# Attention q products in two 64-row halves, and k, v sums placed by one copy, in a one-core attention and expert-routing kernel

## The chip, the core and the metric

One core of one Trainium2 chip runs the whole program. Its engines have a queue each: TensorE (PE in the rows, PEld for its weight loads), VectorE (DVE), ScalarE (ACT), GpSimd (POOL) and SyncE (SP). They wait for one another by semaphores. The metric is the device time of one execution in microseconds, as the median of several.

## What is computed

Eight batches of 576 tokens with eight heads of 64 columns go through a linear attention without softmax; each head's output row is divided by its root mean square and scaled by `g_norm`. The 4608 rows of 512 columns then go to one of eight experts each (the largest gate logit), in the order of the tokens and up to a capacity of 1152 for an expert; an expert is two products with a ReLU between. Rows beyond the capacity stay zero.

```python
kv = np.einsum('bhsd,bhse->bhde', k, v)               # 8, 8, 64, 64
out = np.einsum('bhsd,bhde->bhse', q, kv)             # 8, 8, 576, 64
rms = np.sqrt(np.mean(out * out, axis=-1, keepdims=True) + 1e-06)
x = (out / rms * g_norm)                              # laid out as 4608 x 512
logits = x @ w_gate                                   # 4608 x 8
expert_idx = np.argmax(logits, axis=1)
gate_w = softmax(logits)[np.arange(N), expert_idx]
...                                                   # dispatch in order of tokens, up to capacity
h = np.maximum(np.einsum('ecd,edf->ecf', disp, w1), 0.0)     # F = 1024
y = np.einsum('ecf,efd->ecd', h, w2)
out[i] = gate_w[i] * y[expert_idx[i], pos[i]]         # for each token that was kept
```

## The kernel before, in words

**Stages.** The first part, to about 100 us, is the attention over the eight batches with the routing of each batch behind it; the first expert's weights are loaded and split in the same stretch. The second part, to the end, is the experts: tiles of tokens are gathered (`xg`, `xm`), turned and cast (`xs`), multiplied by w1 (L566), passed through ReLU into a high and a low f16 part (`hh`, `hl`), multiplied by w2 (L613), and scattered into the output (L643). Each expert product is three terms, high by high, high by low and low by high, for which the weights are split into `w1h`, `w1l`, `w2h` and `w2l` (L411 makes the low parts on DVE).

**Attention, by batch.** `load` (S, the queue of loads) brings k and v in two parts each and q in one. `kv_products` (L752 to 805) sums kᵀv of each head over five chunks of tokens: 40 matmuls (L761) for each half of the heads. They leave head 2i in partitions 0 to 63 and head 2i + 1 in partitions 64 to 127 of one PSUM bank `a`. `apart` copies the bank to `kvs`; `turn` (L785) transposes that, `keep` copies it to `kvt`, and `gates` (L794) multiplies it by the gate weights, so that each head gets eight more columns for the routing. The right operand of the q products is `kv_bd` (L300): four pairs of heads, each a block-diagonal 128x144 matrix (72 columns = 64 of kv and 8 of gates for each head), with zeros off the diagonal that GpSimd writes once, at the start (L700). The diagonal blocks are filled by two `spread` copies (64x4x64 each, one for each half of the partitions) and two small copies of the gate columns (64x4x8).

**Units.** A `unit` (L811 to 830) is one chunk of 128 tokens of one batch, five to a batch, 40 in all. It has two halves of four heads: two matmuls of 128 rows by 144 columns into one bank `op` (L822; in f32 each matmul is two passes), and a copy of the 128x288 result to `o_sb` (L826, recorded at the line of the copy itself, L719 for ACT or L721 for DVE). There are four `op` banks, so two units fit. `squares` (L833 to 850) squares the result on ACT (L843) and sums it on DVE into `ss` (L848). When all five chunks of a batch are summed, `route` makes the root mean square (`vh`, `yi`, `nrt`), the logits, the chosen expert (`ohe`) and the running number of each token in its expert: `place` on PE (L965, `misc<-ohe`), and `enter` into the table of slots (`tab`). After the last batch, `count` (L1042, one product on `misc`) gives the tokens of each expert; the order of the experts and the registers of the later gathers come from it.

**What sets the order.** All this is not issued in the order of the code. `Plan.op` takes, for each operation, the engines that may do it with a length on each ("A", 0.29 and "V", 0.34 for a copy of `kvs`; "T", 0.49 for half a unit), its dependencies, a key, and the rotating buffers (`Ring`) that it takes and uses. `Plan.place` is a list scheduler: it repeatedly takes, over all engines, the operation that can start first by these lengths, ties by key, and so decides both engine and order; `emit` issues the instructions in that order. Where the plan leaves PE idle before an operation, `emit` puts in dummy products (`beside`, L694, one for each 0.31 us of idle time in the plan). A length in the plan therefore changes what is issued where, for all engines. The tiles of the first expert come into the same plan; a second plan orders the rest of the experts.

Of the kernel before, what the change touches and what calls it, by code (L numbers as in the profile page):

```python
# [66 lines left out]
LOAD = 1.41  # L67
QLOAD = 2.75
# [106 lines left out]
def attention_moe_kernel(  # L175
# [124 lines left out]
    for i in range(2):  # L300
        kv_bds.append(cst.tile([P, HH, 2, XW], F32, name=f"kv_bd{i}"))
# [397 lines left out]
    for t in kv_bds:  # L699
        nc.gpsimd.memset(t, 0.0)  # L700
# [44 lines left out]
    def kv_products(b, ts):  # L745
# [30 lines left out]
        def spread(g):  # L776

            return op([("A", 0.29), ("V", 0.34)],
                      lambda e: copy(e, kv2[rows[g], :, g, 0:D], ks.t[rows[g]].rearrange("p (i x) -> p i x", i=HH)), done[0:1],
                      key + 1.5, (kv,), (ks,))  # L780
# [19 lines left out]
        done = [spread(g) for g in range(2)]  # L800
        for g in range(2):
            done.append(op([("A", 0.19), ("V", 0.13)],
                           lambda e, g=g: copy(e, kv2[rows[g], :, g, D:XW],
                                               a3.t[rows[g], 0:H * E].rearrange("p (i g x) -> p i g x", g=2, x=E)[:, :, g]),
                           [o] + done[0:2], key + 2, (kv,), (a3,)))
# [5 lines left out]
    def unit(b, n, ts, kv, ready, oh):  # L811
        c, key = CHUNKS[n], b * C + n
        o_sb, done = oh.t, []
        for half in range(2):
            qh, qd = ts["q", 0]
            ph = new("op")

            def product(e, half=half, qh=qh, ph=ph):
                ph.t = bank("op")
                for i in range(2):  # L820
                    q0 = half * CD + (i * MD * 2 + c * P if c else i)
                    nc.tensor.matmul(ph.t[:, i * 2 * XW:(i + 1) * 2 * XW], lhsT=qh.t[:, q0:q0 + P],  # L822
                                     rhs=kv.t[:, 2 * half + i].rearrange("p g x -> p (g x)"), start=True, stop=True)

            def out_(e, half=half, ph=ph):
                copy(e, o_sb[:, c, half * HH:(half + 1) * HH].rearrange("p h x -> p (h x)"), ph.t[:, 0:4 * XW])  # L826

            o = op(("T", 0.49), product, [qd] + ready, key + half * 0.1, (ph,), (qh, kv))
            done.append(op([("A", 0.29), ("V", 0.37)], out_, [o], key + half * 0.1, (oh,), (ph,)))
        return done  # L830
# [883 lines left out]
```

## Time and profile before

| | us |
|---|---|
| median of 3 runs | 535.31 |
| the three runs | 534.57, 535.31, 536.51 |
| profiled execution, its own time | 536.39 |
| span of its instructions | 534.6 |
| PE busy | 514.1 (96%) |
| DVE busy | 372.1 (70%) |
| ACT busy | 243.8 (46%) |
| POOL busy | 167.6 (31%) |
| mean granted TensorE clock | 0.994 |

All rows come from one profiled execution, whose time lies 1.08 us above the median and 1.8 us above its span. Times in the rows are counted from the start of the span. A matmul of the f32 kind stands as two instructions, so a unit of four matmuls is eight. The dummies are counted as busy PE. Weight loads (PEld) overlap products. A copy of a helper that all stages call has the helper's line, so it is told by the names of its tiles. The idle time before a row is printed with what ended it; `issue` there means that the engine waited for nothing that the trace shows, and `remote` that the releaser isn't known.

### The profile page before, as it was taken

Reading aid. Unit: us, or ns where it says so; the run is one execution under the profiler, and the core shown is the slowest. Engines: PE = TensorE matmul, PEld = TensorE weight load, DVE = VectorE, ACT = ScalarE, POOL = GpSimd, SP = SyncE. Lnnn points to the kernel's source line nnn. Section 1 sums busy time; section 2 is a strip of 40 time slices with the busy share of each in tenths; the row PEclk is TensorE's granted clock in tenths of the full one; section 3 lists DMA queues with packets and bytes.
Section 4 is the critical chain, followed back from the end, with each engine's and each line's share of the span. In section 5 each row is a group of like instructions: output and inputs, shape, how many; then the busy total and the mean of one; then the engine's idle time right before and its main releaser. Section 6 shows DMA issues by size and latency. Waiting matters only on the chain.

```text
span 534.6 us, 11557 instructions
## 1 busy us (share of the span) xinstructions
PE 514.1 (96%) x4456; PEld 356.4 (67%) x4456; DVE 372.1 (70%) x999; ACT 243.8 (46%) x482; POOL 167.6 (31%) x173
## 2 busy tenths in 40 slices
PE   8999898999898999999999999999999999999995
PEld 7998887966464665477546755775587478558743
DVE  4488787998598899999998993768297335104800
ACT  1665587993236526547256252625263353112111
POOL 2001002001524652563265406430743353120012
PEclk8999999999999999999999999999999999999999
DMA  8999999722697893974849645555546132010010
GB/s 309 419 420 421 422 419 417 285 101 99 226 303 144 235 274 65 364 190 138 281 138 276 148 132 184 151 151 163 167 144 140 55 93 44 20 45 23 1 40 33
DMA packets 61806, 102.69 MB, mean 192 GB/s; under 512 B 38508, under 2 KB 38508, under 8 KB 59698
## 3 DMA queue, kind: packets, MB, share of 16 engines
q1 hardware_dynamic: 54144, 70.50, 42.4%
q0 software_dynamic: 7584, 31.38, 16.5%
q8 instruction: 37, 0.61, 0.5%
q14 instruction: 23, 0.19, 0.1%
q10 hardware_dynamic: 18, 0.02, 0.0%
HBM read 73.20 MB, written 20.68 MB: 176 GB/s over the span
## 4 chain that ended last, share of the span: by engine, by line
issue 32%; PE 31%; POOL 13%; DVE 11%; DMA 8%; ACT 4%; POOLq 1%; another core or an unknown queue 1%; DVEq 0%; SPq 0%; ACTq 0%
PE yp L613 10%; PE hp L566 9%; DMA v_sb<-in_v_dram 6%; POOL out_dram L643 4%; POOL pair L499 3%; POOL xm L470 3%; PE op L566 3%; PE op L822 2%; POOL xg L462 2%; DMA xg<-x_dram,gi 2%; PE a L761 2%; DVE am L376 2%; PE misc L694 1%; PE yp L622 1%; ACT sq L843 1%
## 5 line engine op out<-in xcount | busy, mean ns | idle before, releaser
L566 PE MATMUL hp<-xs,w1h 128*128 128x320 f16 (+6 forms) x960 | 134.0, 292 | 3.1 <-DVE hl L574 1.5
L566 PEld LDWEIGHTS <-w1h 128*128 128x128 f16 x1024 | 99.5, 98 | 36.9 <-issue 4.9
L643 POOL DMA_INDIRECT out_dram<-ysb,si x42 | 46.7, 1112 | 162.9 <-ACT ysb L638 157.3
L613 PEld LDWEIGHTS <-hh 128*128 128x128 f16 x560 | 54.4, 98 | 62.8
L571 ACT ACTIVATE hh<-hp 128x320 f16<-128x320 f32 (+7 forms) x64 | 41.0, 640 | 105.4 <-PE hp L566 97.0
L376 DVE TENSOR_REDUCE am<-raw 128x1 f32<-128x512 f32 x112 | 70.5, 674 | 4.9 <-DMA raw<-in_moe_w_dram 4.8
L566 PE MATMUL hp<-xs,w1l 128*128 128x320 f16 (+6 forms) x480 | 71.9, 292 | 0.0
L638 ACT ACTIVATE ysb<-yp,ysc 128x512 f32<-128x512 f32 (+5 forms) x41 | 28.1, 684 | 92.3 <-PE yp L613 88.5
L574 DVE SCALAR_TENSOR_TENSOR hl<-hp,hh 128x320 f16<-128x320 f32 (+7 forms) x64 | 47.5, 742 | 29.2 <-ACT hh L571 26.3
L613 PE MATMUL yp<-w2l,hh 128*128 128x512 f16 x272 | 64.6, 379 | 0.0
L613 PE MATMUL yp<-w2h,hh 128*128 128x512 f16 x272 | 64.4, 379 | 0.0
L613 PE MATMUL yp<-w2h,hl 128*128 128x512 f16 x272 | 64.4, 379 | 0.0
L566 PEld LDWEIGHTS <-w1l 128*128 128x128 f16 x512 | 50.0, 98 | 16.6
L462 POOL DMA_INDIRECT xg<-x_dram,gi x42 | 42.4, 1010 | 49.5 <-DVE gt L475 14.3
L411 DVE SCALAR_TENSOR_TENSOR w2l<-raw,sw,w2h 128x512 f16<-128x512 f32 x64 | 54.1, 886 | 1.0 <-ACT w2h L405 1.0
L628 DVE COPY yt<-yp 128x256 f32<-128x256 f32 (+4 forms) x7 | 2.9, 413 | 72.9 <-PE yp L622 63.6
L411 DVE SCALAR_TENSOR_TENSOR w1l<-raw,sg,w1h 128x512 f16<-128x512 f32 x64 | 52.0, 858 | 0.0
L613 PEld LDWEIGHTS <-hl 128*128 128x128 f16 x280 | 27.2, 98 | 34.1 <-issue 1.8
L499 POOL TENSOR_TENSOR pair<-xm,pair 128x512 f16<-128x512 f32 (+5 forms) x27 | 32.2, 1192 | 42.7 <-ACT pair L495 42.4
L405 ACT ACTIVATE w2h<-raw,sw 128x512 f16<-128x512 f32 x64 | 41.3, 711 | 8.7 <-PE yp L622 7.7
L822 PE MATMUL op<-kv_bd,q_sb 128*128 128x144 f32 x320 | 44.0, 290 | 0.2 <-issue 0.2
L405 ACT ACTIVATE w1h<-raw,sg 128x512 f16<-128x512 f32 x64 | 41.3, 712 | 2.3 <-DVE sg L400 2.3
(230 smaller groups left out, 618.7 us busy)
## 6 DMA issues: line engine op xcount, KB each, us to landing
raw<-in_moe_w_dram SPq DMA_DIRECT2D x64, 512.0 KB
in_sb<-in_k_dram SPq DMA_DIRECT2D x16, 576.0 KB
v_sb<-in_v_dram SPq DMA_DIRECT2D x32, 288.0 KB
q_sb<-in_q_dram SPq DMA_DIRECT2D x8, 1152.0 KB
x_dram<-o_sb POOLq DMA_DIRECT2D x8, 720.0 KB
x_dram<-o_sb POOLq DMA_DIRECT2D x8, 576.0 KB
xg<-x_dram,gi POOLq DMA_INDIRECT x42
out_dram<-ysb,si POOLq DMA_INDIRECT x42
```

Of the source, the lines that this page charges most:

```text
L376: nc.vector.tensor_reduce(out=am()[:, p:p + 1], in_=raw[:, sl(p)], axis=AX.X, op=ALU.max, apply_absolute_value=True)
L405: nc.scalar.activation(wh[:, sl(p)], raw[:, sl(p)], AF.Copy, scale=z["s"])
L411: nc.vector.scalar_tensor_tensor(out=wl[:, sl(p)], in0=raw[:, sl(p)], scalar=z["s"], in1=wh[:, sl(p)], op0=ALU.mult, op1=ALU.subtract)
L462: nc.gpsimd.indirect_dma_start(out=self.xg[i][0:n], out_offset=None, in_=x_dram[0:self.rows, :], in_offset=bass.IndirectOffsetOnAxis(ap=se ...
L499: eng.tensor_tensor(out=pair[0:n, 1], in0=self.xm[i][0:n], in1=pair[0:n, 0], op=ALU.subtract)
L566: nc.tensor.matmul(self.view(hp)[:, v], lhsT=w[:, c, f * P:(f + 1) * P], rhs=x[:, c, u * hw:(u + 1) * hw], start=(t == 0 and c == 0), stop ...
L571: nc.scalar.activation(self.out(self.hh, j), self.view(hp), AF.Relu)
L574: nc.vector.scalar_tensor_tensor(out=self.out(self.hl, j), in0=self.view(hp), scalar=0.0, in1=self.out(self.hh, j), op0=ALU.max, op1=ALU.s ...
L613: nc.tensor.matmul(yp[0:n, 0:DM], lhsT=h[:, j, o:o + n], rhs=w[:, j, :], start=(m == 0), stop=(m == len(self.terms) - 1))
L638: nc.scalar.activation(self.ysb[0:n], yp[0:n, 0:DM], AF.Copy, scale=self.ysc[0:n, i:i + 1])
L643: nc.gpsimd.indirect_dma_start(out=(disjoint.pop() if disjoint else out)[:, :], out_offset=bass.IndirectOffsetOnAxis(ap=self.sidx[0:n, col ...
L822: nc.tensor.matmul(ph.t[:, i * 2 * XW:(i + 1) * 2 * XW], lhsT=qh.t[:, q0:q0 + P], rhs=kv.t[:, 2 * half + i].rearrange("p g x -> p (g x)"), ...
```

## The change

- `kv_bd` is now 128x4x72 without the off-diagonal blocks: head 2i of pair i is in partitions 0 to 63, head 2i + 1 in 64 to 127, as `kvs` has them. GpSimd's memsets of it go.
- The two `spread` copies become one, `whole` (128x4x64). The gate columns are still copied by two.
- A unit is one operation on PE instead of two, planned with 0.87 in place of twice 0.49. It has eight matmuls of 64 rows by 72 columns (16 passes), one of the lower and one of the upper half of the partitions in turn; the lower ones go to one bank, the upper ones to another. Each of the two copies out takes one bank, which now holds every second head, so that its destination in `o_sb` is four pieces of 72 columns.

```diff
+UNIT = 0.87
...
-        kv_bds.append(cst.tile([P, HH, 2, XW], F32, name=f"kv_bd{i}"))
+        kv_bds.append(cst.tile([P, HH, XW], F32, name=f"kv_bd{i}"))
...
-    for t in kv_bds:
-        nc.gpsimd.memset(t, 0.0)
...
-        def spread(g):
-
-            return op([("A", 0.29), ("V", 0.34)],
-                      lambda e: copy(e, kv2[rows[g], :, g, 0:D], ks.t[rows[g]].rearrange("p (i x) -> p i x", i=HH)), done[0:1],
-                      key + 1.5, (kv,), (ks,))
+        def whole(e):
+            copy(e, kv2[:, :, 0:D], ks.t.rearrange("p (i x) -> p i x", i=HH))
...
-        done = [spread(g) for g in range(2)]
+        done = [op([("A", 0.29), ("V", 0.34)], whole, done, key + 1.5, (kv,), (ks,))]
         for g in range(2):
             done.append(op([("A", 0.19), ("V", 0.13)],
-                           lambda e, g=g: copy(e, kv2[rows[g], :, g, D:XW],
+                           lambda e, g=g: copy(e, kv2[rows[g], :, D:XW],
                                                a3.t[rows[g], 0:H * E].rearrange("p (i g x) -> p i g x", g=2, x=E)[:, :, g]),
-                           [o] + done[0:2], key + 2, (kv,), (a3,)))
+                           [o] + done[0:1], key + 2, (kv,), (a3,)))
...
-        o_sb, done = oh.t, []
-        for half in range(2):
-            qh, qd = ts["q", 0]
-            ph = new("op")
-
-            def product(e, half=half, qh=qh, ph=ph):
-                ph.t = bank("op")
-                for i in range(2):
-                    q0 = half * CD + (i * MD * 2 + c * P if c else i)
-                    nc.tensor.matmul(ph.t[:, i * 2 * XW:(i + 1) * 2 * XW], lhsT=qh.t[:, q0:q0 + P],
-                                     rhs=kv.t[:, 2 * half + i].rearrange("p g x -> p (g x)"), start=True, stop=True)
-
-            def out_(e, half=half, ph=ph):
-                copy(e, o_sb[:, c, half * HH:(half + 1) * HH].rearrange("p h x -> p (h x)"), ph.t[:, 0:4 * XW])
-
-            o = op(("T", 0.49), product, [qd] + ready, key + half * 0.1, (ph,), (qh, kv))
-            done.append(op([("A", 0.29), ("V", 0.37)], out_, [o], key + half * 0.1, (oh,), (ph,)))
-        return done
+        o_sb, (qh, qd), phs = oh.t, ts["q", 0], (new("op"), new("op"))
+
+        def product(e):
+            for g in range(2):
+                phs[g].t = bank("op")
+            for i in range(HH):
+                q0 = i // 2 * CD + (i % 2 * MD * 2 + c * P if c else i % 2)
+                for g in range(2):
+                    r = slice(g * D, (g + 1) * D)
+                    nc.tensor.matmul(phs[g].t[:, i * XW:(i + 1) * XW], lhsT=qh.t[r, q0:q0 + P], rhs=kv.t[r, i], start=True,
+                                     stop=True)
+
+        def out_(e, g):
+            copy(e, o_sb[:, c, g::2], phs[g].t[:, 0:HH * XW].rearrange("p (i x) -> p i x", i=HH))
+
+        o = op(("T", UNIT), product, [qd] + ready, key, phs, (qh, kv))
+        return [op([("A", 0.29), ("V", 0.37)], lambda e, g=g: out_(e, g), [o], key + g * 0.1, (oh,), (phs[g],)) for g in range(2)]
```

The new lengths and dependencies give the plan another order in the attention stage; behind it the experts' order is the same row for row, as are the loads' on SP throughout. Three places follow, each kernel's instructions in the order in which the engine gets them.

**Order piece 1**, PE, around the last k, v products of batch 7 (`a<-v_sb_82`) and the units of batch 6 (`kv_bd_160`) and 7 (`kv_bd_161`), before:

```order
L761 MATMUL a<-v_sb_82,in_sb_76 64x64 x20
L694 MATMUL misc<-iota_94 128x128 x3
L785 MATMUL a<-ident,kvs 128x128 x2
L694 MATMUL misc<-iota_94 128x128 x2
L794 MATMUL a<-wgs,kvt 128x32 x2
L694 MATMUL misc<-iota_94 128x128 x2
L822 MATMUL op<-kv_bd_160,q_sb_77 128x144 x20
L822 MATMUL op<-kv_bd_161,q_sb_78 128x144 x10
```

and after:

```order
L760 MATMUL a<-v_sb_82,in_sb_76 64x64 x20
L695 MATMUL misc<-iota_94 128x128 x4
L781 MATMUL a<-ident,kvs 128x128 x2
L695 MATMUL misc<-iota_94 128x128 x2
L818 MATMUL op<-kv_bd_160,q_sb_77 128x72 x16
L790 MATMUL a<-wgs,kvt 128x32 x2
L818 MATMUL op<-kv_bd_160,q_sb_77 128x72 x24
L695 MATMUL misc<-iota_94 128x128 x2
L818 MATMUL op<-kv_bd_161,q_sb_78 128x72 x16
L482 MATMUL x<-ident,xm 128x128 x4
```

Two units of batch 6 moved ahead of batch 7's gate products, and other work of PE now lies between the units of batch 6 and 7.

**Order piece 2**, DVE, around the copies of batch 7's k, v sums (`kvs`, `kv_bd_161`) and batch 6's `vh`, before:

```order
L721 COPY o_sb_231<-op 128x288
L848 TENSOR_REDUCE ss_232<-sq 128x8
L411 SCALAR_TENSOR_TENSOR w1l_175<-raw_173,sg,w1h_174 128x512
L848 TENSOR_REDUCE ss_232<-sq 128x8
L411 SCALAR_TENSOR_TENSOR w1l_175<-raw_173,sg,w1h_174 128x512
L872 TENSOR_SCALAR vh<-ss_232 128x40
L721 COPY kv_bd_161<-kvs 64x4x64
L411 SCALAR_TENSOR_TENSOR w1l_175<-raw_173,sg,w1h_174 128x512 x2
L886 TENSOR_TENSOR nrt<-yi,vh 128x40
L721 COPY kv_bd_161<-a 64x4x8
```

and after:

```order
L843 TENSOR_REDUCE ss_230<-sq 128x8
L720 COPY o_sb_229<-op 128x4x72
L843 TENSOR_REDUCE ss_230<-sq 128x8
L720 COPY o_sb_229<-op 128x4x72
L412 SCALAR_TENSOR_TENSOR w1l_175<-raw_173,sg,w1h_174 128x512
L843 TENSOR_REDUCE ss_230<-sq 128x8
L720 COPY kvs<-a 128x256
L843 TENSOR_REDUCE ss_230<-sq 128x8
L412 SCALAR_TENSOR_TENSOR w1l_175<-raw_173,sg,w1h_174 128x512
L867 TENSOR_SCALAR vh<-ss_230 128x40
```

The copy `kvs` moved from ACT to DVE, ahead of `vh`; DVE's copy into `kv_bd_161` is gone, and more `o_sb` copies lie on DVE there.

**Order piece 3**, PE, around batch 7's `place` (`misc<-ohe` with `upto`) and the count (`misc<-ohe` with `ones`), before:

```order
L965 MATMUL misc<-ohe,upto_123 128x8
L1042 LDWEIGHTS ones_117
L1042 MATMUL misc<-ohe,ones_117 128x8
L613 LDWEIGHTS hl
L613 MATMUL op<-w2h_176,hl 128x512
```

and after:

```order
L960 MATMUL misc<-ohe,upto_123 128x8
L695 MATMUL misc<-iota_94 128x128
L1037 LDWEIGHTS ones_117
L1037 MATMUL misc<-ohe,ones_117 128x8
L695 MATMUL misc<-iota_94 128x128 x2
L614 LDWEIGHTS hh
L614 MATMUL op<-w2l_177,hh 128x512
```

The count, which stood behind four products of hh by w2l, now stands ahead of them and of two dummies.

## Rows read from the trace of the kernel before

**Rows 1.** The page, sections 1 and 2: busy times, and DMA by slice.

```profile
PE 514.1 (96%) x4456; PEld 356.4 (67%) x4456; DVE 372.1 (70%) x999; ACT 243.8 (46%) x482; POOL 167.6 (31%) x173
...
DMA  8999999722697893974849645555546132010010
```

**Rows 2.** Windows of 5 us, its header giving the columns, from 90 us.

```profile
core 0: us, PE busy (x) PEld busy (x) DVE busy (x) ACT busy (x) POOL busy (x), PEclk, DMA share, GB/s
...
90.00:95.00 5.00, 3.17 (x26) 2.79 (x25) 2.79 (x9) 3.23 (x9) 1.54 (x2) 1.00 0.88 352
95.00:100.00 5.00, 5.00 (x42) 4.96 (x41) 4.97 (x15) 5.00 (x16) 0.00 (x0) 1.00 0.87 292
```

**Rows 3.** Timeline, PE: start, length, engine, line, tiles, count, [idle before <-releaser].

```profile
82.05 4.16 PE L822 MATMUL op<-kv_bd,q_sb 128*128 128x144 f32 x32
86.14 1.39 PE L761 MATMUL a<-v_sb,in_sb 128*64 128x64 f32 x40
...
88.20 1.39 PE L761 MATMUL a<-v_sb,in_sb 128*64 128x64 f32 x40 [0.68 <-DMA v_sb<-in_v_dram]
...
92.16 0.44 PE L785 MATMUL a<-ident,kvs 128*128 128x128 f32 x2 [1.71 <-ACT kvs L719]
...
93.17 0.63 PE L794 MATMUL a<-wgs,kvt 128*128 128x32 f32 x4
...
94.17 7.78 PE L822 MATMUL op<-kv_bd,q_sb 128*128 128x144 f32 x60
```

**Rows 4.** Groups by form, 0 to 130 us: count, busy us, mean ns, idle before.

```profile
L822 PE MATMUL op<-kv_bd,q_sb 128*128 128x144 f32 x320 | 44.0, 290 | 0.2 <-issue 0.2
L848 DVE TENSOR_REDUCE ss<-sq 128x8 f32<-128x512 f32 x40 | 26.9, 680 | 1.7 <-ACT sq L843 1.2
L761 PE MATMUL a<-v_sb,in_sb 128*64 128x64 f32 x640 | 23.0, 228 | 2.3 <-DMA v_sb<-in_v_dram 2.2
L719 ACT COPY o_sb<-op 128x288 f32<-128x288 f32 x62 | 23.0, 405 | 9.1 <-PE op L822 8.4
L721 DVE COPY o_sb<-op 128x288 f32<-128x288 f32 x18 | 8.1, 453 | 4.6 <-PE op L822 4.4
...
L411 DVE SCALAR_TENSOR_TENSOR w2l<-raw,sw,w2h 128x512 f16<-128x512 f32 x8 | 6.0, 744 | 0.0
```

**Rows 5.** Timeline, DVE, ACT and PE, 84 to 109 us.

```profile
84.04 0.17 DVE L678 COPY gi<-gidx_tab 128x6 int32 x1 [0.35 <-issue]
...
89.56 0.18 DVE L872 TENSOR_SCALAR vh<-ss 128x40 f32<-128x40 f32 x1
...
91.74 0.37 ACT L719 COPY kvs<-a 128x256 f32<-128x256 f32 x1 [2.40 <-remote]
...
92.14 0.28 DVE L721 COPY kv_bd<-kvs 64x256 f32<-64x256 f32 x1 [2.40 <-ACT kvs L719]
...
93.28 0.40 ACT L719 COPY kv_bd<-kvs 64x256 f32<-64x256 f32 x1
...
106.24 0.69 DVE L489 TENSOR_TENSOR xs<-x,xs 128x512 f16<-128x512 f32 x1
...
108.72 0.81 PE L566 MATMUL op<-xs,w1h 128*128 128x384 f16 x4 [0.18 <-ACT xs L719]
```

**Rows 6.** Timeline, DVE and PE, at batch 7's numbering and count.

```profile
128.83 1.03 PE L613 MATMUL op<-w2l,hh 128*128 128x512 f16 x4
128.86 0.24 DVE L946 TENSOR_REDUCE ohe<-ohe 128x8 f16<-128x48 f16 x1
129.95 0.17 PE L1042 MATMUL misc<-ohe,ones 128*128 128x8 f16 x1
130.16 0.20 DVE L971 TENSOR_TENSOR inc<-misc,ohe 128x40 f32<-128x40 f32 x1 [1.06 <-PE misc L1042]
...
131.70 0.83 PE L694 MATMUL misc<-iota 128*128 128x128 f32 x6
...
146.46 1.90 PE L566 MATMUL hp<-xs,w1h 128*128 128x320 f16 x12 [0.46 <-ACT ysb L638]
```

## What is predicted for the changed kernel

> **What bounds the kernel now.** I read the page's busy times and slices first [rows 1]. TensorE (PE) is busy 514.1 of 534.6 us, but in the attention stage, which the change touches, that is no sign of a bound: dummy products fill its gaps there. The DMA slices stand at 8 and 9 for the first six or seven slices of 13.4 us each, so up to about 90 us loading sets the pace, and work that an engine saves there is hidden by the loads as long as their order stays.
>
> Second, the windows after that [rows 2]. From 95 to 100 us VectorE (DVE) is busy 4.97 and ScalarE (ACT) 5.00 of 5.00 us, PE 5.00 as well, while DMA falls to 0.87. What counts is therefore the end of attention: the last two batches, 6 and 7, whose products are copied out of PSUM, squared, summed and routed by ACT and DVE. After that PE works through the experts with few gaps, so a microsecond there is a microsecond at the end, if the routing of batch 7, which the later gathers wait for, moves along.
>
> Third, the timelines of that end. PE finishes the last k, v products at about 89.6 (88.20 plus 1.39) [rows 3], but ACT's copy `kvs` starts at 91.74, after 2.40 us of waiting whose releaser the trace doesn't know; DVE's `kv_bd` waits 2.40 behind it, and PE's transposes 1.71 [rows 3, 5]. From 94.17 PE runs 60 passes of the q products without a gap [rows 3]. The first expert product starts at 108.72, released by ACT's last `xs` [rows 5]. Batch 7's numbering (`ohe` on DVE) ends at 129.10 (128.86 plus 0.24); DVE then waits 1.06 us for PE, which counts at 129.95 only after four w2l products [rows 6].
>
> **The change part by part.** *The q products.* Before, a unit (128 tokens of a batch) is four matmuls of 144 columns, in f32 two passes each, so eight passes: (7.78 - 0.29) / 59 = 0.127 us from start to start, 1.02 us a unit [rows 3, 4]. After, it is eight matmuls of 72 columns, sixteen passes, each on half of the partitions. No row of before shows such halves, so bounds. The pace of one pass with 128 weight columns doesn't fall with its columns: the 32-column gate products run at (0.63 - 0.28) / 3 = 0.117 us [rows 3]. If the halves don't overlap, a unit takes 16 x 0.117 = 1.87 us. If they overlap fully, 8 x 0.117 = 0.94. The nearest row is the k, v product, which runs on two halves of the columns: (1.39 - 0.22) / 39 = 0.030 us a pass, 0.060 for a pair with 64 weight columns [rows 3, 4]; twice that for 128 columns is 0.12 a pair, 0.96 a unit. I take 0.94, because pairs on halves are shown to overlap there; the plan's new constant, 0.87, is near it. Over 40 units that saves PE 40 x 0.08 = 3.2 us, 30 of them under the loads; at the end the ten units of batches 6 and 7 save 0.8 us, on an engine that waits for ACT and DVE there.
>
> Changing between halves and the whole array costs something too: the k, v products start 0.09 us later than the q products' pace would have it (82.05 + 31 x 0.125 + 0.125 = 86.05, and the row says 86.14) [rows 3]. In the new order the last ten units stand in six groups, twelve changes, about 1.1 us, which takes back the 0.8. The Trainium skill, TensorEngine Tiling (Array Packing), Key Properties, says that changing the tiling mode drains TensorE; that 0.09 us agrees with it, and for the new mode no row shows it.
>
> *The copies out.* They stay 80, of 288 elements each: 0.405 us on ACT, 0.453 on DVE [rows 4]. Their destination falls into four pieces; ACT's `kv_bd` copy, also in four pieces, took 0.40 for 256 elements where `kvs`, in one, took 0.37 [rows 5]. So up to 0.03 each, 20 x 0.03 = 0.6 on two engines at the end, 0.3 us at most, and nothing where the other engine is the later one; I take 0.1. Both copies of a unit now wait for the whole unit, but the last copy of one is no later. Here TensorEngine Tiling (Array Packing), PSUM Bottleneck, in the Trainium skill speaks against the change: tiling makes TensorE faster and leaves the evacuation of PSUM as it is. The windows agree, with ACT and DVE full at 95 to 100 us; by that rule alone the saving would be nought, which is nearly what my sum has.
>
> *k and v placed by one copy.* One copy of each batch goes: 0.28 us on DVE or 0.40 on ACT [rows 5]. Seven lie under the loads. The last is in the count below. The memsets on GpSimd that go stand at the start, beside the first loads: nothing. The order on the queue of loads is the same row for row, so nothing is held up there but by the q load of the last batch, which waits for batch 5's units; they are now mixed with k, v products of about 1.4 us, while transfers are still queued ahead of it. I cost that at nothing; without that cover it would be about 1 us.
>
> *The moved work, at the end.* PE now takes batch 6's first units before batch 7's gate products, and `kvs` of batch 7 is now on DVE (order pieces 1, 2). When does DVE reach it? Before, from its `gi` copy at 84.04 to `vh` at 89.56 it does three w1l, four sums and one `o_sb` copy. After, ahead of `kvs` stand two w1l, four sums and five `o_sb` copies: 4 x 0.45 more, 0.75 less [rows 4, 5], so `kvs` at about 89.56 + 1.05 = 90.6, if the unexplained wait doesn't recur, and at 91.74 if it does.
>
> From there to the end of batch 7's `ohe` DVE has 121 instructions before and 121 after. Leaving: the `kv_bd` copy (0.28), two gate copies (an estimate of 0.2 each, small beside the rest), an `o_sb` copy (0.45), one w2l (0.75): 1.9. Coming: `kvs` (0.37), one sum (0.67), an `xs` cast (as the `xs` row, 0.69), two small ones (0.2 each): 2.1 [rows 4, 5]. So the stretch is 129.10 - 92.14 = 36.96 before [rows 5, 6] and 37.2 after, but begins with `kvs` itself, 0.40 earlier than `kv_bd` did. It ends at 90.6 + 37.2 = 127.8, or at 91.74 + 37.2 = 128.9: 1.3 or 0.2 us earlier.
>
> What is late next? PE's count. Before, it stands behind four w2l products (about 0.86 us) and follows `ohe` by 0.85; after, those four and two dummies are behind it, and the three dummies after the hl products (0.66) are gone [rows 6] (order piece 3). So the count follows `ohe` closely, and what was saved ahead of it is paid behind it: 0.86 + 0.44 - 0.66 = 0.64 more up to batch 7's table, against 0.65 less. PE and routing both shift by about 1.3 or 0.2 us. The first expert product has room: up to the count PE has 129.95 - 108.72 = 21.2 us of work, 1.3 less after, so it may start as late as 108 to 109; from `kvs` to it took 17.0 before, with no more on DVE's queue now, so 107.6 or 108.7.
>
> **The sum.** Profiled execution 536.39 us, span 534.6 and 1.8 around it; it lies 1.1 above the median 535.31. 536.39 - 1.3 + 0.1 = 535.2 or 536.39 - 0.2 + 0.1 = 536.3. The wait of 2.1 us at `kvs` has no cause in the trace, and the three runs differ by 1.9, so it may come and go in either kernel; I take the middle, **535.7 us**, no change: within 0.3% of the median, 533.7 to 536.9, which is about what a measurement of this kernel can tell.
>
> **Rivals.**
> *Faster, 533.5.* The wait is a matter of the old order and goes for good, and batch 6's units, no longer behind batch 7's gates, fill ACT and DVE from 90 on: `kvs` at 89.6, a stretch from there to 126.8, 2.3 earlier, and DVE's wait of 1.06 for the count shrinks to the 0.75 of the w2l moved into it, 0.3, with 0.3 of PE's wait before the rest's products (0.46) [rows 6]: 2.9 in all. For it: both engines idle 2.40 us in before. Against: DVE then has as much work as before.
>
> *Slower by the halves, 541.* The halves don't overlap, so the change doesn't do what it says. PE gets to the end of the ten units at about 96.0 + 10u (91.6 after the transposes, and 4.4 of gates, dummies, transposes and changes of mode), and needs 1.1 more to the first expert product. It decides from u = 1.08, where this passes 107.9; at u = 1.87 the product starts at 115.8, the count at 135.7 after 19.9 us of work, 5.7 late at most, some of it given back in later waits: 541. Against it: the k, v pairs overlap.
>
> *Slower by the order, 537.7.* The wait recurs and PE's path is 1 to 1.5 us longer: more changes of mode than I priced, or the two copies of a unit, released together, hold the four banks longer. DVE and ACT then wait in a stretch where nothing has slack. The point is PE's end of the ten units passing DVE's second `xs` sum, 105 to 107, at a unit of about 1.0.
>
> **Chances.** Forecast 0.45; faster 0.33; slower by the order 0.12, by the halves 0.10. So faster 0.33, same 0.45, slower 0.22. The range takes in the faster rival and the milder slower one, with 0.7 and 0.8 around them for the wait that comes and goes: 532.8 to 538.5; the halves stay out. The forecast's own range is 534.8 to 536.9.
>
> **What would show it.** After's rows should have sixteen q passes a unit within 0.87 to 1.0 us, in pairs; more than 1.08 is the halves. `kvs` on DVE at 90.6 (or 91.7), the first expert product at 107 to 109, the count at 127.9 to 129.3, ACT and DVE still full at 95 to 100, and the DMA slices as before. The prediction is wrong if batch 7's numbering moves more than 2 us, or if the loads end later.

## The result, and the profile after

The changed kernel takes 539.19 us (median of 15 runs, 537.12 to 550.76), the kernel before 535.93 us beside it (15 runs). The ratio of the two is 1.0057, with a 95% interval of 1.0033 to 1.0081: slower by 0.6%, some 3 us. A ratio leaves out runs more than 1.5% above the fastest of their kernel (here two of the 15). Forecast were 535.7 us, no change, and 538.5 as the upper end. The profiled execution took 539.08 us, its span is 537.3, its mean granted clock 1.000.

The page of after, busy times and DMA by slice, against [rows 1]: PE is 5.0 us busier, DVE and ACT are as they were.

```profile
PE 519.1 (97%) x4798; PEld 359.1 (67%) x4798; DVE 373.1 (69%) x996; ACT 243.4 (45%) x477; POOL 167.0 (31%) x171
...
DMA  8999998823588793994839647555645132010010
```

Windows of after, same columns and stretch as [rows 2]. DMA falls earlier, 0.77 in the first of them against 0.88. PE is full from 95 us on as before, DVE and ACT, with 4.47 and 4.28, not quite.

```profile
core 0: us, PE busy (x) PEld busy (x) DVE busy (x) ACT busy (x) POOL busy (x), PEclk, DMA share, GB/s
90.00:95.00 5.00, 3.89 (x56) 3.33 (x54) 3.20 (x6) 2.77 (x7) 2.35 (x3) 1.00 0.77 233
95.00:100.00 5.00, 5.00 (x81) 4.76 (x80) 4.47 (x12) 4.28 (x13) 0.00 (x0) 1.00 0.89 314
```

Timeline of after, PE and one row of DVE (start, length, engine, line, tiles, count, idle before), for [rows 3, 5, 6]. L818 are the q products, L760 the k, v products, L695 dummies.

```profile
11.29 2.08 PE L695 MATMUL misc<-iota 128*128 128x128 f32 x8
...
17.76 0.47 PE L818 MATMUL op<-kv_bd,q_sb 64*128 64x72 f32 x4
...
83.08 2.01 PE L818 MATMUL op<-kv_bd,q_sb 64*128 64x72 f32 x32
...
90.03 1.34 PE L760 MATMUL a<-v_sb,in_sb 128*64 128x64 f32 x31
91.70 0.35 PE L760 MATMUL a<-v_sb,in_sb 128*64 128x64 f32 x4 [0.33 <-issue]
...
93.19 0.29 PE L760 MATMUL a<-v_sb,in_sb 128*64 128x64 f32 x2 [0.39 <-issue]
...
95.16 2.01 PE L818 MATMUL op<-kv_bd,q_sb 64*128 64x72 f32 x32
97.10 0.63 PE L790 MATMUL a<-wgs,kvt 128*128 128x32 f32 x4
97.66 2.90 PE L818 MATMUL op<-kv_bd,q_sb 64*128 64x72 f32 x48
100.49 0.71 PE L695 MATMUL misc<-iota 128*128 128x128 f32 x4
101.13 2.13 PE L818 MATMUL op<-kv_bd,q_sb 64*128 64x72 f32 x32
...
110.55 0.66 PE L567 MATMUL op<-xs,w1h 128*128 128x384 f16 x3
...
148.48 1.76 PE L567 MATMUL hp<-xs,w1h 128*128 128x320 f16 x11 [0.46 <-ACT xs L718]
```

```profile
93.52 0.42 DVE L720 COPY kvs<-a 128x256 f32<-128x256 f32 x1 [0.78 <-PE a L760]
```

The halves do overlap: 48 passes in 2.90 us are (2.90 - 0.28) / 47 = 0.056 a pass, 0.89 for a unit. Yet `kvs` of batch 7 starts at 93.52, released by PE, where 90.6 or 91.7 was forecast; batch 6's first unit starts 1.0 us later than in [rows 3], the first expert product 1.8 later and the rest's first product (`hp`) 2.0 later than in [rows 5, 6].

The 2.7 us between the two spans have three places. 1.4 are there already at the first unit, 17.76 against 16.38 in before (below); one program starts as differently from one execution to the next, as the experiments show. 0.6 come between it and `hp` (130.72 us against 130.08). The last 0.7 come behind `hp`, at one gather of the experts. There DVE waits for `xg` and PE for DVE, 3.27 us against 2.32 at DVE. In e10 and e17 below, which have the new products too, that wait is 2.50 and 2.45, so its longer form doesn't come with them each time. PE's and DVE's rows of before for these places, and then of after:

```profile
9.86 2.08 PE L694 MATMUL misc<-iota 128*128 128x128 f32 x8 [0.19 <-DVE wgs L315]
...
16.38 0.85 PE L822 MATMUL op<-kv_bd,q_sb 128*128 128x144 f32 x5
...
80.34 0.66 PE L822 MATMUL op<-kv_bd,q_sb 128*128 128x144 f32 x4
...
167.41 0.15 DVE L475 TENSOR_SCALAR gt<-xg 128x1 f32<-128x1 f32 x1 [2.32 <-DMA xg<-x_dram,gi]
...
170.39 0.22 PE L391 MATMUL pt_max<-diag,ones_b 128*128 128x128 bf16 x1 [1.55 <-DVE diag L388]
```

```profile
170.31 0.15 DVE L476 TENSOR_SCALAR gt<-xg 128x1 f32<-128x1 f32 x1 [3.27 <-DMA xg<-x_dram,gi]
...
173.29 0.22 PE L392 MATMUL pt_max<-diag,ones_b 128*128 128x128 bf16 x1 [2.49 <-DVE diag L389]
```

### The profile page after: what moved, and what is told of

The parts are those of the page before. It is cut to its first block, busy times and chain, and to the rows that moved or that the text cites. A ratio compares the mean times of both kernels' runs of the same rounds, so it can differ in the third digit from the quotient of the medians.

```text
span 537.3 us, 12232 instructions
## 1 busy us (share of the span) xinstructions
PE 519.1 (97%) x4798; PEld 359.1 (67%) x4798; DVE 373.1 (69%) x996; ACT 243.4 (45%) x477; POOL 167.0 (31%) x171
## 4 chain that ended last, share of the span: by engine, by line
PE 38%; issue 31%; POOL 13%; DVE 10%; ACT 5%; DMA 3%; POOLq 1%; ACTq 0%; SPq 0%
PE yp L614 12%; PE hp L567 9%; PE op L818 5%; POOL out_dram L644 4%; PE a L760 4%; POOL xm L471 3%; POOL pair L500 3%; PE op L567 3%; POOL xg L463 2%; PE misc L695 2%; DVE am L377 2%; DVE w2l L412 2%; DMA xg<-x_dram,gi 1%; DVE hl L575 1%; ACT sq L838 1%
## 5 line engine op out<-in xcount | busy, mean ns | idle before, releaser
L639 ACT ACTIVATE ysb<-yp,ysc 128x512 f32<-128x512 f32 (+5 forms) x41 | 28.1, 684 | 91.7 <-PE yp L614 82.6
L818 PE MATMUL op<-kv_bd,q_sb 64*128 64x72 f32 x640 | 41.5, 276 | 0.0
```

The lines of the kernel that those rows point to most:

```text
L639: nc.scalar.activation(self.ysb[0:n], yp[0:n, 0:DM], AF.Copy, scale=self.ysc[0:n, i:i + 1])
L818: nc.tensor.matmul(phs[g].t[:, i * XW:(i + 1) * XW], lhsT=qh.t[r, q0:q0 + P], rhs=kv.t[r, i], start=True, stop=True)
```

## The experiments

The first question was which part of the change costs the time: the order or the products. The kernels that bear on it, with the dummies in the whole trace (before has 79) and the range of the runs' mean granted clocks (half clock for 10.7 of 537 us makes a mean of 0.99):

| kernel | products | dummies | runs | clock | median us | ratio to before |
|---|---|---|---|---|---|---|
| after | halves | 90 | 15 | 0.972 to 1.000 | 539.19 | 1.0057 [1.0033, 1.0081] |
| e5, after again | halves | 90 | 6 | 0.984 to 0.993 | 541.49 | 1.0094 [1.0076, 1.0111] |
| e1 | whole | 90 | 12 | 0.995 to 1.000 | 537.29 | 1.0008 [0.9984, 1.0032] |
| e16, e1 again | whole | 90 | 11 | 0.991 to 1.000 | 537.87 | 0.9996 [0.9968, 1.0025] |
| e17 | halves | 76 | 5 | 0.978 to 0.999 | 538.03 | 1.0112 [1.0066, 1.0157] |
| e18 | whole | 76 | 11 | 0.992 to 0.998 | 533.07 | 1.0022 [1.0008, 1.0035] |
| e10 | halves | 115 | 5 | 0.993 to 0.999 | 536.37 | 1.0065 [1.0052, 1.0079] |
| e3 | halves, planned 0.94 | 77 | 12 | 0.968 to 0.987 | 547.78 | see below |
| e9 | whole, planned 0.94 | 77 | 11 | 0.993 to 0.999 | 532.65 | 0.9996 [0.9985, 1.0007] |
| e11 | halves, planned 0.94 | 101 | 11 | 0.991 to 1.000 | 534.24 | 1.0029 [1.0019, 1.0039] |

Ratios are to the kernel before on the same chip in the same session (536.48 us for e1 to e4, 536.18 for e5 to e8, 532.75 for e9 to e12, 538.48 for e13 to e16, 532.28 for e17 and e18).

**e1 and e16: the new order with the old products.** The products and copies of before, planned as one operation of 0.87 with both `spread` copies in one, which gives after's order.

```diff
...
-            for i in range(HH):
-                ...
-                for g in range(2):
-                    nc.tensor.matmul(phs[g].t[...], lhsT=qh.t[r, q0:q0 + P], rhs=kv.t[r, i], ...)
+            for half in range(2):
+                ...
+                for i in range(2):
+                    nc.tensor.matmul(phs[half].t[...], lhsT=qh.t[:, q0:q0 + P],
+                                     rhs=kv.t[:, 2 * half + i].rearrange("p g x -> p (g x)"), ...)
...
```

> The products, the zeros and the two copies of k, v of the kernel before, but planned as the changed kernel plans them (one operation of 0.87 a unit, one for both copies), so that PE, DVE and ACT get their work in the changed kernel's order. If the order is the cause (batch 5's units behind the diag and tab products, k, v products of batch 7 ending late), this is slow like the changed kernel: ratio 1.004 to 1.008 to before, first unit of batch 5 at about 83, kvs of batch 7 at 93 to 94.5. If the new form of the products and copies is the cause, it is as fast as before: 0.998 to 1.002, with kvs at 91.7 or earlier.

> The old products in the new order once more, as the base of e13 and e14 on the same chip: 1.000 to 1.003 of before, clock at least 0.99.

1.0008 and 0.9996: the order by itself costs nothing that 23 runs can tell, at most 0.3% by the intervals, and no theory that puts all of the 0.6% down to the order survives. The two profiles also show what a start can be worth. The same kernel has its first unit at 17.90 us in e1 and at 14.42 in e16, and `hp` at 149.72 and 146.12: here 3.5 us of start arrive whole. PE does its first work more slowly in e1: ten dummies (twenty passes) take 4.63 us against 3.95, four 2.08 against 1.16, and twenty k, v products 2.05 against 1.39, though the granted clock reads 1.00 in both; the cause isn't shown. Over all 20 profiles the first unit starts between 14.2 and 19.9 us, with whole and half products alike. In the old order a late start isn't seen at the end: e7, before and e12 have first units at 14.66, 16.38 and 18.25 and `hp` at 146.10, 146.46 and 145.36. At nearly the same start and at full clock, after's execution took 539.08 us (17.76, clock 1.000) and e1's 539.59 (17.90, 0.999), so one execution doesn't show the loss of the median. PE's rows of e1 and then of e16:

```profile
1.70 4.63 PE L695 MATMUL misc<-iota 128*128 128x128 f32 x20 [1.70 <-POOL iota L231]
...
10.87 2.08 PE L695 MATMUL misc<-iota 128*128 128x128 f32 x8
12.87 2.05 PE L762 MATMUL a<-v_sb,in_sb 128*64 128x64 f32 x40
...
17.90 2.23 PE L819 MATMUL op<-kv_bd,q_sb 128*128 128x144 f32 x16
```

```profile
1.69 3.95 PE L695 MATMUL misc<-iota 128*128 128x128 f32 x20 [1.69 <-POOL iota L231]
...
8.97 1.16 PE L695 MATMUL misc<-iota 128*128 128x128 f32 x8 [0.18 <-DVE wgs L316]
10.06 1.39 PE L762 MATMUL a<-v_sb,in_sb 128*64 128x64 f32 x40
...
14.42 2.23 PE L819 MATMUL op<-kv_bd,q_sb 128*128 128x144 f32 x16
...
95.55 3.19 PE L819 MATMUL op<-kv_bd,q_sb 128*128 128x144 f32 x24
98.58 0.61 PE L695 MATMUL misc<-iota 128*128 128x128 f32 x4
```

**e13 and e14: one product more in a unit.** On top of e16's kernel, in e13 of 64 rows (a change into halves and back), in e14 of 128 rows (no change), into columns of the bank that nobody reads. The added lines of e13; e14 has `0:P` for both `0:D`.

```diff
...
+                if half == 0:
+                    nc.tensor.matmul(phs[0].t[:, 4 * XW:5 * XW], lhsT=qh.t[0:D, 0:P], rhs=kv.t[0:D, 0, 0], start=True, stop=True)
...
```

> The kernel with the old products in the new order (e1), with one product more ahead of each unit's four: 64 rows by 72 columns into columns of the bank that nobody reads, so that PE changes to halves and back 40 times, ten of them in the last ten units. Order and plan are those of e1. Theory (the changes between halves and the whole array are the new form's price): the profile's starts show about 0.22 for its two passes, which have no partner on the other half, and about 0.24 more for going in and out, 0.4 to 0.46 a unit where PE doesn't wait, 4 to 4.5 us over the last ten; time about 1.006 to 1.009 of before, and 0.003 to 0.005 above the same kernel with a product of 128 rows. Rival (only the clock makes the new form slower, the changes are hidden): no difference from the kernel with a product of 128 rows, both 1.003 to 1.006, unless the granted clock falls below 0.99.

> As e13, but the added product has all 128 rows, by 72 columns, so nothing changes its mode: two passes of about 0.12, 0.23 us a unit, 2.3 us over the last ten if PE is the path there throughout. Both theories: 1.003 to 1.006 of before; 1.001 if PE is not the path there.

Batch 6's last three units, PE's timeline in e14 and then in e13, beside the x24 row of e16 above and the x48 row of after:

```profile
103.56 0.42 PE L818 MATMUL op<-kv_bd,q_sb 128*128 128x72 f32 x2
...
107.26 0.61 PE L695 MATMUL misc<-iota 128*128 128x128 f32 x4
107.70 0.34 PE L818 MATMUL op<-kv_bd,q_sb 128*128 128x72 f32 x2
```

```profile
111.91 0.44 PE L818 MATMUL op<-kv_bd,q_sb 64*128 64x72 f32 x2
...
116.46 0.61 PE L695 MATMUL misc<-iota 128*128 128x128 f32 x4
```

From these to the next dummies three units take 3.03 us in e16, 3.70 in e14, 4.55 in e13 and 2.83 in after. So the whole product costs 0.22 a unit, and going into halves and back 0.28 on top of it. After's own rows agree with such a price: from the start of two dummies (four passes) to the next units it takes 0.64 us (100.49 to 101.13), and 0.44 in e14 (107.26 to 107.70), where both are whole. The times were 537.87 (e16), 545.62 (e14, 1.0126 [1.0087, 1.0165]) and 556.25 (e13, 1.0349 [1.0314, 1.0384]), all at a clock of 0.991 or more. 40 x 0.22 = 8.9 us of added work moved the end by 7.8, 40 x 0.28 = 11.3 us of changes by 10.6; in the traces, from the first unit to `hp`, it is 6.2 and 11.3. Both theories had expected far less, the last ten units alone. So in the new order nearly all of the work that is added to the units, under the loads too, arrives at the end.

**e5: after once more**, unchanged.

> The changed kernel once more, on the chip and in the hour of the three next ones, so that they can be set against it. 1.003 to 1.008 of before. If the wait of the k, v products of batch 7 belongs to this place in the program, it is there again: they end 1.5 us or more after their usual pace would have it.

541.49 us, 1.0094 [1.0076, 1.0111], with two of six runs below 0.99: slower again, and by more. The profiled run (0.984, 544.34 us) shows what a lost clock can cost the unchanged program. Two of its windows, and then the same two of after:

```profile
40.00:50.00 10.00, 9.75 (x100) 9.30 (x102) 5.18 (x18) 4.60 (x10) 0.97 (x2) 0.53 1.01 420
50.00:60.00 10.00, 9.99 (x134) 9.42 (x135) 5.48 (x24) 3.67 (x12) 1.08 (x2) 0.79 1.02 421
```

```profile
40.00:50.00 10.00, 10.00 (x164) 9.48 (x162) 8.55 (x31) 6.53 (x17) 1.07 (x2) 1.00 1.01 418
50.00:60.00 10.00, 9.58 (x175) 9.12 (x172) 8.28 (x36) 6.17 (x19) 1.08 (x2) 1.00 1.03 425
```

From the first unit to batch 6's first it takes 85.95 us, after's execution at full clock 77.40. Batch 6's first unit comes 5.4 us later than in after, though the first unit of all came 3.2 earlier.

**e17 and e18: fourteen dummies fewer** in the whole program, 76 where before has 79, with the new and the old products.

```diff
-BESIDE = 0.75
+BESIDE = 0.65
```

> The changed kernel with 12 dummies fewer (75 in place of 87 between the products of the attention), which is as many as the kernel before has, the order of everything else the same. Theory (PE's queue is the path through the attention in this order, so fixed work on it counts): at full clock some 12 x 0.25 = 3.0 us less on PE, 1.5 to 2.5 us of it seen at the end: 1.001 to 1.003 of before. Rival (with products on half of the rows the clock falls unless dummies keep it up): clock below 0.985 in half of the runs or more, 1.010 to 1.020.

> The old products in the new order, with the same 12 dummies fewer. Theory (PE's queue is the path): 1.5 to 2.5 us less than with them, 0.995 to 0.997 of before, if the clock holds. Rival (the dummies lie in waits and cost nothing): 1.000. If the clock falls below 0.985 here as well, what brings it down is not the halves.

The clock held with whole products and not with halves: e17 has 0.978, 0.982, 0.983 and 0.987 in four of five runs, at 541.5 to 534.4 us; its fifth, at 0.999, took 533.4, which is e18's time. The rival was right for e17. For e18 it was the dummies that lie in waits: no gain, 0.2% slower. So fourteen dummies are not like e14's products, which arrive. The profiles of both are at full clock (0.999 and 0.997), and from the first unit to batch 6's first e17 takes 78.55 us, e18 77.54.

**e10, e11 and e12: more dummies** in after, in e3's kernel and in the kernel before.

```diff
-BESIDE = 0.75
+BESIDE = 0.95
```

> The changed kernel with more dummy products in the plan's idle time of PE (BESIDE 0.95 in place of 0.75: 115 dummies in place of 90), everything else in the same order. Clock theory: the stretches at half clock get fewer, mean clock 0.996 or more as the median (0.992 before this), and the time comes down to what is left at full clock, 537.5 to 539, ratio 1.002 to 1.006. If the clock doesn't depend on how much PE does there: clock and time as in the changed kernel, 1.006 to 1.010; if the dummies get in the way of real work, slower than that.

> UNIT 0.94, the new products, and BESIDE 0.95 (101 dummies in place of 77). Clock theory: fewer runs with a long stretch at half clock than 9 of 12, and a median of 534 to 539. Otherwise 546 to 549 as the median, as without them.

> The kernel before with BESIDE 0.95 (100 dummies in place of 79), as the control for the two runs ahead. Its clock is high already; 0.998 to 1.003, a mean clock as before's or somewhat higher. If dummies cost time by standing ahead of real work, this shows it: over 1.003.

The clock comes back: 0.993 or more in e10, 0.991 or more in e11. The loss stays: both are slower than the kernel before with the clock kept, 1.0065 and 1.0029, while e9 below, whole products in e11's order, stands at 0.9996. In the kernel before itself (e12) 21 dummies more cost nothing, 1.0000 [0.9990, 1.0011]; what e11's 24 more than e9's cost in their own order wasn't measured.

**e3 and e9: a unit planned with 0.94**, near its measured length, with half and with whole products (e9 is e1's kernel with it); the order is the same in both.

```diff
-UNIT = 0.87
+UNIT = 0.94
```

> The changed kernel with UNIT 0.94 in place of 0.87, which gives an order near that of before: one unit of batch 5 ahead of diag, two behind it, then tab, then the last two, then k and v of batch 7 in one piece. Order theory: about as before or a little better, 0.996 to 1.002, kvs of batch 7 at 90 to 92. Form theory: 1.004 to 1.007.

> The products, zeros and copies of the kernel before, planned with one operation of 0.94 a unit, so that all queues have the order of the run with UNIT 0.94, where the new products mostly lost 27 us to half clock from 94 us on. If the new products are what lets the clock fall, it stays up here: mean clock 0.99 or more in nearly all runs and 0.995 to 1.002 of before. If the order, with its idle time of PE at kvs of batch 7, lets it fall, most runs lie at 0.97 and 545 us or more, as there.

This is the clearest pair for the clock. All 12 runs with halves are below 0.99. Eight take 547.1 to 549.0 us and four 535.8 to 540.9, whose ratio is 1.0019 [0.9971, 1.0067]; two of these, at a clock of 0.985, took 535.82 and 536.05, no more than the kernel before (536.48), so a lost clock isn't always lost time. All 11 with whole products are at 0.993 or more, with a ratio of 0.9996. The two ran in different sessions, with clocks of 0.988 to 0.999 and 0.991 to 1.000 for the kernel before. Windows of e3 and then of e9, columns as above:

```profile
90.00:95.00 5.00, 2.84 (x43) 2.58 (x39) 1.58 (x4) 1.50 (x6) 2.02 (x3) 0.93 0.93 361
95.00:100.00 5.00, 5.00 (x39) 4.78 (x40) 4.31 (x12) 2.84 (x8) 0.00 (x0) 0.50 0.31 67
100.00:105.00 5.00, 5.00 (x45) 4.64 (x44) 3.27 (x9) 2.86 (x8) 0.00 (x0) 0.50 0.86 309
...
115.00:120.00 5.00, 5.00 (x38) 4.36 (x37) 2.21 (x6) 2.95 (x9) 0.00 (x0) 0.50 0.01 3
```

```profile
90.00:95.00 5.00, 5.00 (x42) 4.82 (x42) 4.56 (x13) 4.05 (x12) 0.51 (x1) 1.00 0.85 349
95.00:100.00 5.00, 4.58 (x35) 4.11 (x35) 5.00 (x18) 4.85 (x15) 0.00 (x0) 1.00 0.78 257
```

In e3 PE had been busy 2.84 of 5 us, then ran at the lower of its two levels, 1.2 GHz, to beyond 120 us, although its busy time is 5.00 of 5.00 us all the while. The first expert product starts at 121.77 there and at 106.98 in e9.

**e15: dummies in halves.** After, with dummies of the lower 64 rows, so that no change lies between dummies and units.

```diff
-        nc.tensor.matmul(misc[:, 384:512], lhsT=iota128, rhs=iota128, start=True, stop=True)
+        for r in (slice(0, D),):
+            nc.tensor.matmul(misc[:, 384:512], lhsT=iota128[r], rhs=iota128[r], start=True, stop=True)
```

> The changed kernel, but a dummy is a product of the lower 64 rows by 128 columns in place of 128 rows, so that no change lies between the dummies and the q products; a dummy still takes two passes of about 0.11. Three or four groups of dummies between the last ten units lose two changes each. Theory of the changes: the stretch from batch 6's first unit to the last unit is 0.5 to 0.9 us shorter than the 13.0 of the changed kernel, if the clock stays full. Theory of the clock (products on half of the rows bring it down): more half-clock stretches than in the changed kernel, clock below 0.985 in most runs, and the time 1.01 or more.

560.8 us, 1.045 [1.0395, 1.0505], clock 0.945 to 0.967 in all four runs. Fewer changes, more halves: the clock decides. Where it is full, from 115 us on, the changes that are gone do show: three units and two dummies take 3.23 us (117.19 to 120.42 below), 3.47 in after (97.66 to 101.13). But from batch 6's first unit to the end of batch 7's last it is 13.09 against 13.30, 0.2 less where 0.5 to 0.9 was expected. A window and PE's timeline of e15:

```profile
95.00:100.00 5.00, 4.62 (x37) 3.90 (x35) 2.48 (x11) 1.33 (x2) 0.00 (x0) 0.50 0.38 159
```

```profile
117.19 2.90 PE L819 MATMUL op<-kv_bd,q_sb 64*128 64x72 f32 x48
119.93 0.65 PE L696 MATMUL misc<-iota 64*128 64x128 f32 x4
120.42 2.38 PE L819 MATMUL op<-kv_bd,q_sb 64*128 64x72 f32 x32
```

**e4: the halves not in turn.** The eight passes of the lower half, then those of the upper.

```diff
-            for i in range(HH):
+            for g, i in [(g, i) for g in range(2) for i in range(HH)]:
...
-                for g in range(2):
+                for g in (g,):
...
```

> The changed kernel with the eight matmuls of a unit in another order: all four of partitions 0 to 63 first, then all four of 64 to 127, so that neighbours lie on the same half. If halves overlap only when they alternate, a unit takes 16 times 0.11, 1.8 us instead of 0.89, the five units of batch 5 end 3 to 5 us later, and the ratio to before is 1.012 to 1.02 (542 to 547). If the array overlaps them in any order, a unit stays at 0.9 and the time at 1.004 to 1.008.

Two units take 2.63 us in place of 2.01, as here in e4, and the clock falls to 0.943 to 0.949: 574.67 us, 1.0681 [1.0625, 1.0737]. A pass takes (2.63 - 0.28) / 31 = 0.076 us, between the 0.056 in turn and the 0.117 of a pass of the gate products. So the full overlap needs the alternation; a part of it stays without.

```profile
28.58 2.63 PE L818 MATMUL op<-kv_bd,q_sb 64*128 64x72 f32 x32
```

**e2: two units of batch 5 ahead of the nine dummies** before the `diag` product, to undo the delay of batch 7's k, v products. In the emitted order, `moved` are these units and the first one's copies:

```diff
...
+            moved, before = MOVED["moved"], MOVED["before"]
+            todo = [o for o in todo if o not in moved]
+            n = todo.index(before)
+            todo[n:n] = moved
...
```

> The changed kernel with one thing moved: the first two units of batch 5 go ahead of the diag product on PE, and the first one's two copies ahead of w1h on ACT. Order theory: the two units start at 79 to 81 in place of 83.1, kvs of batch 7 comes 1.5 to 2.5 us earlier than 93.5, the last q load is issued 1 to 3 us earlier than 91.1, and the ratio to before is 0.998 to 1.002. Form theory: nothing of that helps, 1.004 to 1.007. A third reading, that a stall of PE at the k, v products of batch 7 costs the time, expects kvs at 93 still.

543.48 us, 1.0123 [1.0084, 1.0163]. PE waited 0.97 us for the q load, the dummies behind it ran at half clock (18 passes in 4.21 us, 2.27 in after), and batch 7's products came later still.

**e6, e7 and e8: the early gathers of `xg` after batch 7's `kvs`.** Before and after, PE waits around batch 7's k, v products while GpSimd issues three gathers; these kernels issue them later (after, before, and e3's kernel), behind a copy of one element of `kvs` on GpSimd.

```diff
...
+            moved = MOVED["fetches"]
+            todo = [o for o in todo if o not in moved]
+            n = todo.index(MOVED["apart"]) + 1
+            todo[n:n] = moved
...
+                nc.gpsimd.tensor_copy(seen, MOVED["ks"].t[0:1, 0:1])
...
```

> The changed kernel, but GpSimd issues the three early gathers of x only after kvs of batch 7 (a one-element copy of kvs on GpSimd stands ahead of them); all other queues keep their order. In all traces so far the k, v products of batch 7 are held for about 2 us while these gathers are issued, and not where they come after them. If the gathers hold them: no hold, kvs at 91.3 to 92 in place of 93.5, and 1.5 to 2.5 us less than the changed kernel, ratio to before 0.999 to 1.004. If the hold is of another origin (code loading, the loads), kvs stays at 93.5 and the ratio at 1.004 to 1.008.

> The same with the kernel before. If the gathers hold PE: kvs at 89.6 to 90.3 in place of 91.74, 1.5 to 2.5 us less than before, ratio 0.995 to 0.998; the difference between the two forms of the kernel then stays at 2 to 3 us, so the hold is not what made the changed one slower. If not: 0.998 to 1.003 and kvs at 91.7.

> UNIT 0.94 (order near that of before) and the gathers behind kvs. With UNIT 0.94 alone PE stood idle for 3 to 4 us at kvs of batch 7 and most runs then had 27 us at half clock from 94 us on. If that idle time is what lets the clock fall, then with it gone the stretch at half clock is gone: mean clock 0.985 or more in nearly all runs and 0.993 to 1.000 of before. If the new products by themselves let it fall, most runs stay at 0.97 and 545 us or more.

In e6 the k, v products then run at their usual pace, but PE is held behind them, beside the gathers (1.42 us before a unit): 1.0247 [1.0207, 1.0286], with a clock of 0.964 to 0.981. In e7 nothing is held, sixty passes of the units take 7.79 us as in [rows 3], but PE waits 1.45 us for the last v load ahead of the k, v products, 0.68 in before, and the time is the same: 0.9994 [0.9971, 1.0017]. e8 gave 1.0142 [1.0109, 1.0175] at 0.974 to 0.989: PE's idle time at `kvs` is gone in its trace, and the clock is lost earlier instead (a mean of 0.935 from the first unit to batch 6's first). In e9 to e12 the gathers lay beside the k, v products and nothing was held. So gathers are not enough to explain the hold of about 2 us, and its cause stays open. Before's profile has it too, 2.1 us between the end of these products and `kvs`, so it isn't what the change cost.

## Why the prediction was wrong, point by point

**Right.** A unit of sixteen passes takes 0.89 us (0.94 forecast), so the rival of halves that don't overlap fell. The copies out are no dearer in four pieces, 399 ns on ACT and 455 on DVE against 405 and 453 in [rows 4], as these groups of after up to 130 us show. The count follows `ohe` closely, and the DMA slices are nearly those of before.

```profile
L718 ACT COPY o_sb<-op 128x288 f32<-128x288 f32 x57 | 20.8, 399 | 8.4 <-PE op L818 8.0
L720 DVE COPY o_sb<-op 128x288 f32<-128x288 f32 x23 | 10.4, 455 | 6.6 <-PE op L818 6.4
```

**The step that failed: the moved work at the end.** The only large term of the sum was 1.3 or 0.2 us gained by it, and it rests on `kvs` of batch 7 at 90.6 or 91.74. I timed that by the instructions ahead of it on DVE. It waits for PE: batch 5's first unit starts at 83.08 in place of 80.34, behind the dummies and `diag`, and its later units stand between batch 7's k, v products. So `kvs` came at 93.52, the first expert product at 110.55 (107.6 or 108.7 forecast), batch 7's count at 130.80 (127.9 to 129.3) and `hp` 2.0 later than before. Counted from the first unit, which takes the later start out, `hp` is still 0.6 later where the sum had it 1.2 or 0.1 earlier. This says why the gain didn't come. It isn't the whole loss: e1 and e16 have the new order and lose nothing.

**A term that was put at nothing: the clock.** Every term was made at full clock, since the profile of before shows 1.00 in this stretch. Pairs with the same order show that products in halves lose the clock more often: 6 of 21 runs of after below 0.99 and none of 23 of e1 and e16; 4 of 5 and none of 11 (e17, e18); 12 of 12 and none of 11 (e3, e9). The kernel before has 4 of 97 such runs in the sessions of e1 to e18. e5's trace shows what it can cost, 8.6 us ahead of batch 6. But it is the smaller part of the measured difference: eleven of after's 15 runs are at 0.991 or more, and their median, 538.68, is still 2.75 us above before's 535.93; the other four move the median by 0.5. e10 and e11 agree, slower with the clock kept. Why halves bring the clock down isn't shown. e15, where dummies on half of the rows brought it further down, speaks for the rows that a product uses, but no row tells the two kinds of busy time apart.

**The mis-sized term: the changes.** I took 0.09 for one, 0.18 in and out; in and out cost 0.28 by e13 and e14. The 0.09 was read where units meet k, v products, which is another change. By "TensorEngine Tiling (Array Packing), Key Properties" in the Trainium skill a change drains TensorE; the runs agree and give it this price. At the end it outweighs the shorter passes by a little more than forecast: from batch 6's first unit to the first expert product after takes 15.39 us, e1 and e16 both 14.90, so 0.5 lost where I had 0.3.

**A reading that went too far: PE's busy time as "no sign of a bound".** For the dummies it holds: e18 has fourteen fewer and gains nothing, e12 has 21 more and loses nothing. For the units it doesn't: of e14's added work 7.8 of 8.9 us arrived. So PE's sum had to be made over 40 units, not over ten. What the 30 under the loads give back stays unclear: from the first unit to batch 6's first, after takes 77.4 us, e1 78.9 and e16 78.8, which would be some 1.4 us gained at full clock, but e17 takes 1.0 more than e18.

**The start of the sum.** I set out from the profiled execution, 1.1 us above the median that I forecast. From the median, 535.31, the same terms give 534.7, further off still.

**The rivals.** "Slower by the order, 537.7" had the right side and a part of the mechanism, changes of mode, with the wrong place: e1 clears the order. None had the clock.

**What stays open.** Why after is 2.75 us slower than before in runs that kept the clock. Its seven runs with a clock of 0.996 or more have a median of 538.7, e1's eleven such runs 537.2. Rows show 0.5 of this at the last ten units. At the late gather e5 and e6 wait as long as after (3.21 and 3.35 us at DVE), e10 and e17 don't. A single profile can't close the sum, since the start alone moves it by up to 3.5 us. No version here is faster than the kernel before: the best, e9, e7 and e12, can't be told from it.

## What to carry to other kernels

Before calling a saving hidden, add one product to the loop and see how much of it arrives at the end: here 7.8 of 8.9 us did, in a stretch where dummies in waits could come and go without a trace. Time a step by the queue that it waits for, not by the one that it stands in. Splitting a product into row halves pays by the pass and costs by the group, 0.28 us in and out here, so count the groups over the whole program. And compare the granted clock of all runs, not of the one that is profiled, and then the runs that kept it: after's profile shows 1.000, a quarter of its runs are below 0.99, and the others are still slower.

## What the runs showed of the hardware

- TensorE's granted clock can be at half while its busy time is 5.00 of 5 us for five windows on end (e3, 95 to 120 us), where the same order with whole products stays at 1.00 (e9).
- Half products overlap fully only in turn: 0.056 us a pass, and two units in 2.01 us against 2.63 with the halves apart.
- A 64-row product between 128-row products costs 0.28 us more than a 128-row one in its place (e13, e14).
- At the start PE runs four dummies (eight passes) in 1.16 or in 2.08 us from one execution to the next; in e16 and e1, the same program, the first unit starts at 14.42 and 17.90, and the spans are 534.2 and 537.8 us.
